# A list scheduler in the builder of an attention and two-layer feed-forward kernel

## The chip, the core and the metric

The kernel runs on one core of a Trainium2 chip. The time is that of one execution on the device, in microseconds (us); the median of 3 runs of the kernel before is 934.12 us (933.48 to 934.25). Engines in the profile: PE is TensorE's matmuls and PEld its weight loads, DVE is VectorE, ACT is ScalarE, POOL is GpSimd, SP is SyncE, which here issues every DMA. Each engine works through its own instructions in the order in which they were written, and waits on semaphores for the others.

## What is computed

Attention with a window of 32 keys to each side and 32 global tokens, for 4 batches and 8 heads of width 64; then a gated layer with an RMS norm in front (width 512, inner width 1536), and a second layer with a squared relu (inner width 2048). There are 2304 tokens. All is f32.

```python
s_ll = np.where(mask, scale * q_l @ k_l.T, -1e9)      # |i - j| <= 32
a_l = softmax(concat([scale * q_l @ k_g.T, s_ll]))
out_l, out_g = a_l @ concat([v_g, v_l]), softmax(scale * q_g @ k_all.T) @ v_all
xn = x / sqrt(mean(x * x) + 1e-6) * rms_g
x = (silu(xn @ w_gate) * (xn @ w_val)) @ w_out
h = x @ w_in
out = (s * relu(h) ** 2 + b) @ w_out2
```

## The kernel before, in words

**Groups.** The tokens are worked in 5 groups, three of 512 and two of 320 (one batch each; then halves of batch 3 with the global tokens of two batches). For each group, layer one has 12 blocks g (gate), 12 blocks v (value) and 12 blocks o (out), and layer two 16 blocks i and 16 blocks p. A block is 4 slices of 3 matmuls (`mm3`, lines 751 to 758), since each operand is split into a high and a low fp32r half: high weights by high input (line 752), high by low (753), low by high (754). A slice of 128x512 comes out in PSUM: g, v and i go to one of two banks `m`, o and p add up in four banks `acc0` to `acc3`.

**What follows a block.** In layer one, ACT makes `sg` = silu of g (line 829), DVE multiplies it with v (`a`, line 841), ACT casts the high half `h` (line 156), and DVE makes the low half (line 162). In layer two, ACT makes `r` = relu (line 858), DVE `t` (859), ACT the high half of `h` (861), DVE the low half (862). The block o or p that reads `h` stands one block i, or one g and v, later on PE. At the end of layer one, ACT and DVE carry the four `acc` to `y` (lines 787, 789).

**Weights.** Each pair of two blocks is 1 MB. There are 34 pairs. In group 0 each comes as raw 64-bit data into one of 4 buffers `wr` (line 174), and is converted by three ACT instructions (`ce` line 205, `cv` line 195, the cast `wt` line 223) and four of DVE (lines 206, 208, 209, 224). Most are then stored to DRAM (`wsc`, line 218), from where the later groups load them (line 279) into one of 7 buffers `wt`; 10 of the 34 are converted again in group 1 instead (`AGAIN`).

**Attention and norm beside it.** While a group runs through its layers, the attention of the next one is computed between the blocks, two heads' pairs at a time (`pair_steps`): scores `st_s`, global scores `st_g`, exponentials `st_e`, transposes `st_t` and `st_tg`, values `st_v`, all through one PSUM bank pair `at`. Then `build_steps` makes the next group's input `x`: squares, `root` (one over the root by a start value and four Newton steps, 15 small DVE instructions in `inv_rms`, lines 495 to 501), the scaling `u` (527) and the transposes `turn`; in two groups also `gsq` and `gnorm`, which do the same for the global tokens on 128x64.

**What sets the order.** The builder writes blocks in a fixed sequence. Between slices `tick` takes a step of attention, of the building or of the conversions when a count of matmul time (`sched["t"]`) has gone past a pace or a lag given with the step; a step is written whole. In group 0 the framework's own scheduler then arranges PE, ACT and DVE with priorities (`hp`) and a few pinned rows (`in_line`), so that slices of different blocks are mixed; from group 1 on (line 812) the written order is the order. SP's order is the order of the calls.

Of the kernel before, what the change touches and what calls it, by code (L numbers as in the profile page):

```python
# [21 lines left out]
T = B * ST  # L22
# [47 lines left out]
W_LEAD = 5  # L70
C_LEAD = 4
# [5 lines left out]
def attn_moe_kernel(ctx: ExitStack, tc: tile.TileContext, q, k, v, w, cst, out):  # L77
# [63 lines left out]
    slots = []  # L141
    for gi in range(len(GROUPS)):
        slots += [(1, gi, f) for f in range(F1)] + [(2, gi, f) for f in range(F2)]
    wt, wraw, wsc, left = {}, {}, {}, {}
    raws, stores = {}, {}
    nraw = [0]
    nload = [PAIRS]
    cnt = {}

    def pick(key, opts):  # L150
        cnt[key] = cnt.get(key, -1) + 1
        return opts[cnt[key] % len(opts)]

    def cpy(e, out_, in_):
        if e == "A":
            A.copy(out=out_, in_=in_)
        else:
            V.tensor_copy(out=out_, in_=in_)

    def hl(dst_h, dst_l, src, eh):  # L160
        cpy(eh, dst_h, src)
        return V.tensor_tensor(out=dst_l, in0=src, in1=dst_h.bitcast(F32), op=ALU.subtract)

    def w_tile(n):
        wt[n] = w_p.tile([128, 2, 2, 512], F32R, tag="w", name="wt")
        left[n] = 2
        return wt[n]

    def load_raw():
        if nraw[0] < len(RAW):  # L170
            n = RAW[nraw[0]]
            nraw[0] += 1
            wraw[n] = wr_p.tile([128, 2, 512], I64, tag="wr", name="wr")
            raws[n] = nc.sync.dma_start(out=wraw[n], in_=w[n % PAIRS])
# [6 lines left out]
    table = []  # L181

    def tabled(xs):
        in_line(table + xs)
        table[:] = [xs[-1]]

    def conv_begin(n, halves=False):
        raw = wraw.pop(n)
# [24 lines left out]
    def keep(n, wn):  # L213
        m = n % PAIRS
        if n == m and m in AGAIN:
            return
        wsc[m] = dr_p.tile([128, 2, 2, 512], F32, name=f"wsc{m}")
        stores[n] = nc.sync.dma_start(out=wsc[m], in_=wn.bitcast(F32))
# [9 lines left out]

    def conv(n):
        g, a, d = conv_begin(n)  # L230
        in_line(a)
        for c, y in (("A", a[0]), ("V", d[0])):
            if c in recent:
                in_line([recent[c], y])
        conv_end(n, g)

    def conv_steps(n):
        raw = wraw.pop(n)
        hi = raw.bitcast(I32).rearrange("p j (n t) -> p j n t", t=2)[:, :, :, 1]
        odd = raw.bitcast(I16).rearrange("p j (n t) -> p j n t", t=2)[:, :, :, 1]  # L240
        e = cv_p.tile([128, 2, 512], I32, tag="cv", name="ce")
        g = cv_p.tile([128, 2, 512], F32, tag="cv", name="cv")
        t = g.bitcast(I32)
        wn = w_tile(n)

        def end():
            V.tensor_tensor(out=wn[:, :, 1], in0=g, in1=wn[:, :, 0].bitcast(F32), op=ALU.subtract)
            load_raw()
            keep(n, wn)

        return [(lambda: A.mul(out=g, in_=hi.bitcast(F32), mul=W_SC), 0.0),
                (lambda: A.copy(out=e.bitcast(I16), in_=odd), 1.3),
                (lambda: V.tensor_scalar(out=g, in0=g, scalar1=-W_HI * W_SC, scalar2=W_HI * W_SC, op0=ALU.max,
                                         op1=ALU.min), 0.6),
                (lambda: V.tensor_scalar(out=e, in0=e, scalar1=13, scalar2=-0x7FFFFFF9, op0=ALU.arith_shift_right,
                                         op1=ALU.bitwise_and), 1.3),
                (lambda: V.scalar_tensor_tensor(out=t, in0=t, scalar=3, in1=e, op0=ALU.logical_shift_left,
                                                op1=ALU.bitwise_or), 0.6),
                (lambda: A.copy(out=wn[:, :, 0], in_=g), 1.3), (end, 1.3)]

    def block(gi, b):
        n, j = divmod(gi * 2 * PAIRS + PLACE[b], 2)
        return n, wt[n][:, j]

    def used(n):
        left[n] -= 1
        if left[n]:
            return
        del wt[n], left[n]
        if n + C_LEAD < PAIRS:  # L270
            conv(n + C_LEAD)
        elif n + W_LEAD in RAW[PAIRS:]:
            sched["c"] += conv_steps(n + W_LEAD)
        while PAIRS <= nload[0] <= n + W_LEAD and nload[0] < PAIRS * len(GROUPS):
            m = nload[0]
            nload[0] += 1
            if m in RAW:
                continue
            nc.sync.dma_start(out=w_tile(m).bitcast(F32), in_=wsc[m % PAIRS])

    ut, og_t, raw_u = {}, {}, {}

    def u_tile(b):
        if b not in ut:
            ut[b] = u_p.tile([128, 4, DM], F32, tag="u", name="u")
        return ut[b]

    def og_tile(b):
        if b not in og_t:
            og_t[b] = xg_p.tile([128, 2, 64], F32, tag=f"xg{b}", name="og")  # L290
        return og_t[b]

    def load_qk(i):
        if i >= len(UNITS) or i in raw_u:
            return
# [5 lines left out]
        for t, src, e in ((qr, q, n), (kr, k, m)):  # L301
            d = nc.sync.dma_start(out=t[:, 0:e], in_=src[b, p, :, 0:e])
            if i < 2:
                in_line([raws[4], d])
# [645 lines left out]
```

## Time and profile before

| what | us |
|---|---|
| median of 3 runs | 934.12 |
| the profiled execution | 934.58 |
| its span, first to last instruction | 932.8 |
| PE busy | 912.6 (98%) |
| DVE busy | 470.4 (50%) |
| ACT busy | 423.0 (45%) |
| DMA, share of 16 engines (main queue) | 72.9% |
| granted TensorE clock, mean | 0.998 |

The first 40 us are the attention of the first group, which has nothing to hide it; it is written by the same lines before and after. From 39.8 us on the blocks run: group 0 to 253 us, group 1 to 465, group 2 to 675, group 3 to 807, group 4 to the end. A row of a timeline gives start, duration, engine, line, operation, what it writes and reads, and in brackets the idle time of the engine ahead of it with what ended it. Matmuls overlap: a 128x512 one is shown with 0.39 us and the next begins 0.23 us after it.

### The profile page before, as it was taken

What the parts mean: (1) busy time and instruction counts of PE and PEld (TensorE: products, weight loads), DVE (VectorE), ACT (ScalarE), POOL (GpSimd) and SP (SyncE); (2) the same over time, 40 slices, a digit from 0 to 9 for tenths busy, and PEclk for the clock granted to TensorE, in tenths of its full rate; (3) what the DMA queues carried; (4) which work ended last, traced back from release to release, by engine and by line L of the source; (5) the groups of instructions that cost most, each with busy time, mean ns of one, the idle gap of its engine ahead of it and who ended that gap; (6) DMA issues with size and microseconds to landing.
All of it is one profiled execution on the core that took longest, in us unless ns stands there. A gap on an engine that the chain in (4) does not pass through costs nothing.

```text
span 932.8 us, 16385 instructions
## 1 busy us (share of the span) xinstructions
PE 912.6 (98%) x6942; PEld 778.0 (83%) x6942; DVE 470.4 (50%) x794; ACT 423.0 (45%) x600; POOL 0.6 (0%) x7
## 2 busy tenths in 40 slices
PE   9899998998999999999999999999999999999998
PEld 7677786877878878788778878887899999999998
DVE  5897999979563563556341242344322135311333
ACT  3797987978436336454214115232232233211322
POOL 0000000000000000000000000000000000000000
PEclk9999999999999999999999999999999999999999
DMA  9799999788958887574666654554588787698780
GB/s 362 290 422 420 350 371 389 248 352 328 350 183 329 309 318 269 189 285 181 225 237 225 254 189 183 192 195 156 204 314 298 280 298 272 246 335 308 289 294 29
DMA packets 43960, 255.77 MB, mean 274 GB/s; under 512 B 5104, under 2 KB 9456, under 8 KB 15984
## 3 DMA queue, kind: packets, MB, share of 16 engines
q1 hardware_dynamic: 43888, 254.73, 72.9%
q8 instruction: 55, 0.90, 0.4%
q14 instruction: 17, 0.14, 0.0%
HBM read 214.60 MB, written 40.11 MB: 273 GB/s over the span
## 4 chain that ended last, share of the span: by engine, by line
PE 77%; ACT 9%; DVE 8%; DMA 3%; issue 2%; POOL 0%; ACTq 0%; DVEq 0%; POOLq 0%
PE m L752 14%; PE m L753 13%; PE m L754 13%; PE acc L753 9%; PE acc L752 9%; PE acc L754 9%; ACT ce L205 2%; DMA wr<-in_w_dram 2%; ACT cv L195 2%; PE at L366 1%; DMA wsc<-wt 1%; ACT h L861 1%; DVE t L859 1%; DVE wt L224 1%; ACT wt L223 1%
## 5 line engine op out<-in xcount | busy, mean ns | idle before, releaser
L753 PE MATMUL acc<-h,wt 128*128 128x512 f32 (+1 forms) x536 | 192.9, 360 | 1.1 <-DVE h L862 1.1
L754 PE MATMUL acc<-h,wt 128*128 128x512 f32 (+1 forms) x536 | 191.6, 358 | 0.0
L752 PE MATMUL acc<-h,wt 128*128 128x512 f32 (+1 forms) x536 | 187.1, 363 | 3.7 <-ACT h L861 3.6
L752 PE MATMUL m<-x,wt 128*128 128x512 f32 (+1 forms) x480 | 174.2, 363 | 0.7 <-ACT sg L829 0.7
L754 PE MATMUL m<-x,wt 128*128 128x512 f32 (+1 forms) x480 | 171.7, 358 | 0.0
L753 PE MATMUL m<-x,wt 128*128 128x512 f32 (+1 forms) x480 | 171.5, 357 | 0.0
L752 PE MATMUL m<-y,wt 128*128 128x512 f32 (+1 forms) x320 | 115.4, 361 | 6.2 <-DVE t L859 6.2
L753 PE MATMUL m<-y,wt 128*128 128x512 f32 (+1 forms) x320 | 115.1, 360 | 1.6 <-DVE y L789 1.6
L752 PEld LDWEIGHTS acc<-h,wt 128*128 128x128 f32 x536 | 100.4, 188 | 18.9 <-ACT h L861 5.2
L754 PE MATMUL m<-y,wt 128*128 128x512 f32 (+1 forms) x320 | 114.8, 359 | 0.0
L753 PEld LDWEIGHTS acc<-h,wt 128*128 128x128 f32 x536 | 100.7, 188 | 15.4 <-DVE h L862 3.1
L754 PEld LDWEIGHTS acc<-h,wt 128*128 128x128 f32 x536 | 100.6, 188 | 12.8 <-issue 0.2
L841 DVE TENSOR_TENSOR a<-sg,m 128x512 f32<-128x512 f32 (+1 forms) x60 | 36.3, 605 | 144.5 <-PE m L754 131.8
L859 DVE SCALAR_TENSOR_TENSOR t<-m,ct,r 128x512 f32<-128x512 f32 (+1 forms) x80 | 53.3, 668 | 105.9 <-ACT r L858 105.3
L752 PEld LDWEIGHTS m<-x,wt 128*128 128x128 f32 x480 | 90.0, 188 | 14.2 <-issue 1.4
L754 PEld LDWEIGHTS m<-x,wt 128*128 128x128 f32 x480 | 90.1, 188 | 11.6
L753 PEld LDWEIGHTS m<-x,wt 128*128 128x128 f32 x480 | 90.1, 188 | 10.9 <-DVE x L604 0.2
L858 ACT ACTIVATE r<-m 128x512 f32<-128x512 f32 (+1 forms) x80 | 42.4, 532 | 120.3 <-PE m L754 119.8
L829 ACT ACTIVATE sg<-m 128x512 f32<-128x512 f32 (+1 forms) x60 | 32.0, 534 | 126.7 <-PE m L754 126.6
L861 ACT ACTIVATE h<-t,ct 128x512 fp32r<-128x512 f32 (+1 forms) x79 | 52.3, 662 | 60.5 <-DVE t L859 58.2
L862 DVE SCALAR_TENSOR_TENSOR h<-t,ct,h 128x512 fp32r<-128x512 f32 (+1 forms) x79 | 53.1, 672 | 47.1 <-ACT h L861 43.3
L752 PEld LDWEIGHTS m<-y,wt 128*128 128x128 f32 x320 | 60.2, 188 | 14.6 <-DVE t L859 7.2
(163 smaller groups left out, 1032.2 us busy)
## 6 DMA issues: line engine op xcount, KB each, us to landing
wt<-wsc SPq DMA_DIRECT2D x126, 1024.0 KB, 4.9
wr<-in_w_dram SPq DMA_DIRECT2D x44, 1024.0 KB, 7.7
wsc<-wt SPq DMA_DIRECT2D x34, 1024.0 KB, 8.3
vr<-in_v_dram SPq DMA_DIRECT2D x12, 1105.0 KB, 8.3
fk<-in_k_dram SPq DMA_DIRECT2D x12, 784.0 KB, 6.0
fq<-in_q_dram SPq DMA_DIRECT2D x12, 272.0 KB, 6.5
out_dram<-z SPq DMA_DIRECT2D x12, 256.0 KB, 4.8
s_v<-in_v_dram SPq DMA_DIRECT2D x2, 1040.0 KB, 9.8
```

The source lines that it names most:

```text
L195: mul = lambda: A.mul(out=g, in_=hi.bitcast(F32), mul=W_SC)
L205: a = [A.copy(out=e.bitcast(I16), in_=odd), mul()]
L223: a = A.copy(out=wn[:, :, 0], in_=g)
L752: mms = [PE.matmul(out_, lhsT=wh, rhs=xh, start=first, stop=False), PE.matmul(out_, lhsT=wh, rhs=xl, start=False, stop=False), PE.matmul(o ...
L753: PE.matmul(out_, lhsT=wh, rhs=xl, start=False, stop=False),
L754: PE.matmul(out_, lhsT=wl, rhs=xh, start=False, stop=last)]
L829: recent["A"] = A.activation(out=sg[:, :N], in_=gb[:, :N], func=AF.Silu)
L841: V.tensor_tensor(out=a[:, :N], in0=sg[:, :N], in1=vb[:, :N], op=ALU.mult)
L858: A.activation(out=r[:, :N], in_=hb[:, :N], func=AF.Relu)
L859: V.scalar_tensor_tensor(out=t[:, :N], in0=hb[:, :N], scalar=ct[:, C_S:C_S + 1], in1=r[:, :N], op0=ALU.mult, op1=ALU.mult)
L861: recent["A"] = A.activation(out=h[:, 0, :N], in_=t[:, :N], func=AF.Identity, bias=ct[:, C_B:C_B + 1])
L862: recent["V"] = V.scalar_tensor_tensor(out=h[:, 1, :N], in0=t[:, :N], scalar=ct[:, C_B:C_B + 1], in1=h[:, 0, :N].bitcast(F32), op0=ALU.add ...
```

## The change

All of `pick`, `conv`, `conv_steps`, `pair_steps`, `build_steps`, `tick`, `emit_step` and the loop over blocks goes. In their place the builder makes a list of operations (`Op`) for all five groups, each with an engine, a duration in us written into the code, what it waits for, and which buffers it takes and frees (`Ring`). Then a loop takes, again and again, the operation that can start first on PE, ACT, DVE or the DMA queue, by these written durations, and writes it; from the end of the first attention on the written order is the order on all four. `cls` ranks what is ready: 0 for what follows a block, then attention and norm (1.0), conversions (2.0, or 0.5 when their pair is at most 3 pairs ahead of PE); no more than 5 pairs ahead. On ACT and DVE an operation of lower rank is left aside if one of rank 0 would be ready over 1 us (`TOL`) before its end. PE takes blocks in a fixed sequence in halves of 6 matmuls, and between halves an attention step that is ready. The Newton steps of the norm are five operations of three instructions each. On SP, raw loads rank before loads from `wsc`, and stores last.

```diff
-W_LEAD = 5
-C_LEAD = 4
+CAP = 4.0
+AHEAD = 5
+CONV = 2.0
+TOL = 1.0
+NEAR = 3
...
+    def commit(o, t):
...
+        x = o.fn()
...
+        free[o.eng] = t + d - OVER[o.eng]
+        o.done = t + d + LAT[o.eng]
...
+        return Op("Q", 2.6, f, [], [r], cls=1.0, after=[prev]), r
...
+    def mm3(out_, wh, wl, xh, xl, fst, lst):
+        r = PE.matmul(out_, lhsT=wh, rhs=xh, start=fst, stop=False)
+        PE.matmul(out_, lhsT=wh, rhs=xl, start=False, stop=False)
+        PE.matmul(out_, lhsT=wl, rhs=xh, start=False, stop=lst)
+        return r
...
+            o = Op("PE", 2 * mm_us(N), f, pairs[n].ops + h["ops"], recs if f_ == 0 else [],
+                   [pairs[n].w, h["rec"]] + ([] if f_ == 0 else recs))
...
+        def f1():
+            x = V.scalar_tensor_tensor(out=T["t"], in0=T["r"], scalar=-0.5, in1=T["r"], op0=ALU.mult, op1=ALU.mult)
+            V.tensor_tensor(out=T["t"], in0=T["t"], in1=T["m"], op=ALU.mult)
+            V.scalar_tensor_tensor(out=T["r"], in0=T["t"], scalar=1.5, in1=T["r"], op0=ALU.add, op1=ALU.mult)
+            return x
+
+        o = Op("V", 3 * us, f0, deps, [], uses)
+        for _ in range(4):
+            o = Op("V", 3 * us, f1, [o])
+        return o, T
...
+        for x in sorted((x for x in c if x[0] <= t0 + 0.6), key=lambda x: (x[1] if x[0] <= t0 + 0.12 else 5 + x[0], x[2])):
...
+            if k > 0 and any(y[0] > s and y[0] < s + d - TOL for y in crit):
+                continue
+            best = x
+            break
...
+        if a and e:
+            if a[0] <= free["PE"] + 0.05 and a[0] >= s["ok"]:
+                return a
+            if e[0] > free["PE"] + 0.3 and a[0] + 0.4 < e[0]:
+                return a
+            return e
...
+    ctx.enter_context(tc.manual_schedule(engines={x.engine for x in (PE, A, V, nc.sync)}))
...
+        E, (t, _, _, o) = min(c, key=lambda x: x[1][0])
...
+        commit(o, t)
```

Three places in the written order show it. The first is DVE in layer two of group 3, where `gnorm` makes the norm of the global tokens (`msq`, `nt`, `r_` are its small tiles, `t` and `h_` those of a block i). Before, its last part:

```order
L501 SCALAR_TENSOR_TENSOR r_7359<-nt,r_7359 128x64
L499 SCALAR_TENSOR_TENSOR nt<-r_7359 128x64
L500 TENSOR_TENSOR nt<-nt,msq 128x64
L501 SCALAR_TENSOR_TENSOR r_7359<-nt,r_7359 128x64
L562 TENSOR_TENSOR gxn<-at,r_7359 128x256
L564 TENSOR_TENSOR gxn<-gxn,ct 128x256
L162 TENSOR_TENSOR x<-gxn,x 128x4x64
L859 SCALAR_TENSOR_TENSOR t<-m,ct,r 128x320
```

The change, at the same norm:

```order
L1073 SCALAR_TENSOR_TENSOR r_7039<-nt,r_7039 128x64
L802 SCALAR_TENSOR_TENSOR t<-m,ct,r 128x320
L1071 SCALAR_TENSOR_TENSOR nt<-r_7039 128x64
L1072 TENSOR_TENSOR nt<-nt,msq 128x64
L1073 SCALAR_TENSOR_TENSOR r_7039<-nt,r_7039 128x64
L810 SCALAR_TENSOR_TENSOR h_7068<-t,ct,h_7068 128x320
L1071 SCALAR_TENSOR_TENSOR nt<-r_7039 128x64
L1072 TENSOR_TENSOR nt<-nt,msq 128x64
```

`t` and the low half of `h` now stand between Newton steps; before, all 18 instructions of the norm stood in one piece.

The second is DVE at the end of layer one of group 0 (`y` is layer two's input, `mx` and `pm_` belong to attention scores, `ce`, `cv`, `wt` to conversions). Before:

```order
L224 TENSOR_TENSOR wt<-cv,wt 128x2x512
L350 TENSOR_TENSOR at<-at,ct 128x16x32
L351 TENSOR_REDUCE mx<-at 128x8
L789 TENSOR_TENSOR y<-acc,y 128x512 x2
L352 TENSOR_TENSOR pm_106<-at,mx 128x1024
L789 TENSOR_TENSOR y<-acc,y 128x512 x2
```

The change:

```order
L536 TENSOR_SCALAR ce<-ce 128x1024
L545 SCALAR_TENSOR_TENSOR cv<-cv,ce 128x1024
L720 TENSOR_TENSOR y<-acc,y 128x512 x4
L553 TENSOR_TENSOR wt<-cv,wt 128x2x512 x2
L540 TENSOR_SCALAR cv<-cv 128x1024
```

The four parts of `y` are now in one piece, with nothing of attention ahead of them or between them.

The third is PE at the first block o of group 0, the first reader of weight pair 2. Before, the framework put the high weights of all four slices first and the low ones (line 754) after the next block had begun:

```order
L752 MATMUL acc<-h,wt 128x512
L753 MATMUL acc<-h,wt 128x512
L752 MATMUL m<-x,wt 128x512
L753 MATMUL m<-x,wt 128x512
L754 MATMUL acc<-h,wt 128x512 x4
```

The change:

```order
L647 MATMUL acc<-h,wt 128x512
L648 MATMUL acc<-h,wt 128x512
L649 MATMUL acc<-h,wt 128x512
L215 MATMUL at<-fk,fq 32x128 x32
L647 MATMUL acc<-h,wt 128x512
L648 MATMUL acc<-h,wt 128x512
```

The third matmul of each slice now reads the low weights, ahead of the next slice; before, eight matmuls with the high weights came first.

## Rows read from the trace of the kernel before

**Rows 1.** From the page: busy time of each engine, and shares of the chain.

```profile
PE 912.6 (98%) x6942; PEld 778.0 (83%) x6942; DVE 470.4 (50%) x794; ACT 423.0 (45%) x600; POOL 0.6 (0%) x7
...
PE 77%; ACT 9%; DVE 8%; DMA 3%; issue 2%; POOL 0%; ACTq 0%; DVEq 0%; POOLq 0%
```

**Rows 2.** Busy time by stretch: PE, PEld, DVE, ACT, POOL, granted clock, DMA share, GB/s.

```profile
39.78:152.44 112.66, 111.91 (x898) 89.24 (x896) 100.80 (x135) 95.17 (x96) 0.00 (x0) 1.00 0.98 396
152.44:252.60 100.16, 92.61 (x581) 74.93 (x580) 81.96 (x127) 79.30 (x91) 0.00 (x0) 0.98 0.85 319
```

**Rows 3.** Waits of PE: line waited for, us in total, times, longest us.

```profile
PE m L752 <- DVE t L859: 6.2, 3, 3.1
PE acc L752 <- ACT h L861: 3.6, 3, 1.8
PE m L753 <- DVE y L789: 1.6, 2, 1.4
PE acc L753 <- DVE h L862: 1.1, 5, 0.3
...
PE m L752 <- ACT sg L829: 0.7, 2, 0.4
```

**Rows 4.** Timeline of PE, matmuls at waits and behind them.

```profile
208.13 0.50 PE L752 MATMUL m<-y,wt 128*128 128x512 f32 x1 [2.00 <-DVE t L859]
...
233.32 0.50 PE L752 MATMUL m<-y,wt 128*128 128x512 f32 x1 [3.14 <-DVE t L859]
233.65 0.39 PE L753 MATMUL m<-y,wt 128*128 128x512 f32 x1
233.88 0.40 PE L754 MATMUL m<-y,wt 128*128 128x512 f32 x1
...
235.13 0.63 PE L752 MATMUL m<-y,wt 128*128 128x512 f32 x1
235.56 0.63 PE L753 MATMUL m<-y,wt 128*128 128x512 f32 x1
...
373.88 0.50 PE L753 MATMUL m<-y,wt 128*128 128x512 f32 x1 [0.19 <-DVE y L789]
...
644.09 0.49 PE L752 MATMUL acc<-h,wt 128*128 128x512 f32 x1 [1.83 <-ACT h L861]
```

**Rows 5.** Timeline of DVE, the norm of global tokens in group 2.

```profile
636.85 0.22 DVE L495 TENSOR_SCALAR msq<-at 128x64 f32<-128x64 f32 x1 [4.21 <-PE at L559]
...
640.42 0.23 DVE L501 SCALAR_TENSOR_TENSOR r<-nt,r 128x64 f32<-128x64 f32 x1
...
642.53 0.75 DVE L859 SCALAR_TENSOR_TENSOR t<-m,ct,r 128x512 f32<-128x512 f32 x1
```

**Rows 6.** Timeline of ACT and DVE ahead of the wait at 233 us.

```profile
230.87 0.59 ACT L858 ACTIVATE r<-m 128x512 f32<-128x512 f32 x1
...
231.73 0.88 DVE L527 TENSOR_SCALAR u<-u,r 128x512 f32<-128x512 f32 x2
```

**Rows 7.** Groups by line and shape, ACT and DVE: busy, mean ns; idle before.

```profile
L205 ACT COPY ce<-wr 128x2048 int16<-128x2048 int16 x31 | 58.8, 1896 | 0.0
L195 ACT ACTIVATE cv<-wr 128x1024 f32<-128x1024 f32 x34 | 39.2, 1153 | 0.6 <-DMA wr<-in_w_dram 0.6
L223 ACT CAST wt<-cv 128x1024 fp32r<-128x1024 f32 x34 | 35.8, 1053 | 6.2 <-DVE cv L209 6.1
...
L829 ACT ACTIVATE sg<-m 128x512 f32<-128x512 f32 x36 | 21.5, 598 | 74.7 <-PE m L754 74.6
...
L224 DVE TENSOR_TENSOR wt<-cv,wt 128x1024 fp32r<-128x1024 f32 x34 | 41.5, 1220 | 4.1 <-ACT wt L223 4.0
```

**Rows 8.** Timeline of ACT: the last cast of the head.

```profile
41.05 1.07 ACT L223 CAST wt<-cv 128x1024 fp32r<-128x1024 f32 x1
```

**Rows 9.** Timeline of PE in the head: an attention step behind its copy.

```profile
30.37 0.32 PE L366 MATMUL at<-s_w,ptf 128*32 128x65 f32 x8 [0.25 <-ACT ptf L676]
```

**Rows 10.** DMA issues: KB each, median us to landing.

```profile
wr<-in_w_dram SPq DMA_DIRECT2D x44, 1024.0 KB, 7.7
```

More of the change, by code (lines that the diff above doesn't have):

```diff
@@ L227, in conv_end @@
         return a, d
[L229 to L279, printed above, removed]
@@ new lines, in attn_moe_kernel @@
+    pool_ = {"A": [], "V": [], "Q": []}
+    free = {"PE": 0.0, "A": 2.0, "V": 4.0, "Q": 5.0}
+    tab = ["S"]
+    first = {}
+    ends = {}
+    def commit(o, t):
+        d = o.dur
+        if o.tab and o.tab != tab[0]:
+            d += 1.28
+            tab[0] = o.tab
+        for r in o.takes:
+            r.ring.hist.append(r)
+        x = o.fn()
+        if o.eng in first:
+            in_line([first.pop(o.eng), x[0] if isinstance(x, list) else x])
+        free[o.eng] = t + d - OVER[o.eng]
+        o.done = t + d + LAT[o.eng]
+        for r in o.uses:
+            r.n -= 1
+            r.t = max(r.t, o.done)
+        for s in o.succ:
+            s.need -= 1
+            s.ready = max(s.ready, o.done)
+        for s in o.then:
+            s.need -= 1
+        if o.eng != "PE":
+            pool_[o.eng].remove(o)
@@ new lines, in load_op, with f, head_pairs @@
+    def load_op(n, prev):
+        p = Pair()
+        p.w = rec("w")
+        def f():
+            wt[n] = w_p.tile([128, 2, 2, 512], F32R, tag="w", name="wt")
+            return nc.sync.dma_start(out=wt[n].bitcast(F32), in_=wsc[n % PAIRS])
+        p.alloc = Op("Q", 2.6, f, [stored[n % PAIRS]], [p.w], cls=1.5, after=[prev])
+        p.ops = [p.alloc]
+        return p
+    def head_pairs():
+        for n in range(2):
+            p = Pair()
+            p.w = rec("w")
+            R["w"].hist.append(p.w)
+            p.ops, p.alloc, p.begin = [], None, None
+            wt[n] = wt_head[n]
+            wsc[n] = wsc_head[n]
+            pairs[n] = p
+        wraw.update(raw_head)
@@ new lines, in all_pairs @@
+    def all_pairs():
+        head_pairs()
+        raw = {}
+        for n in range(6):
+            r = rec("wr")
+            R["wr"].hist.append(r)
+            raw[n] = (None, r, (-9.0, -9.0, -9.0, -5.0, 0.5, 3.5)[n])
+            if n < 2:
+                r.t = 0.0
+        last = None
+        prev = []
+        for n in range(2, PAIRS * len(GROUPS)):
+            if n in RAW:
+                if n not in raw:
+                    o, r = raw_op(n, last)
+                    last = o
+                    raw[n] = (o, r, -9.0)
+                o, r, t = raw[n]
+                p = conv_ops(n, o, r, [pairs[n - 1].begin if n - 1 in pairs and n - 1 > 1 and n - 1 in RAW else None,
+                                       pairs[n - 1].alloc])
+                p.begin.ready = max(p.begin.ready, t)
+                store_op(n, p)
+            else:
+                p = load_op(n, pairs[n - 1].alloc)
+                p.begin = None
+            pairs[n] = p
@@ L875, in _masks @@
+    assert state["e"] == len(experts) and state["a"] == len(attend) and not any(pool_.values())
 def _masks():
```

1039 lines of the change are left out of this document (652 added, 387 removed).

## The prediction

> **What bounds the kernel now.** I read the shares and the chain first [rows 1]. PE is busy 98% of the span, and 77% of the chain runs over it; DVE and ACT are busy 50% and 45%. So the time is the sum of the matmuls, which the change leaves as they are, and of what PE loses between them. DVE and ACT matter only where they let PE wait. The view by stretch shows where that is likely: in layer one of group 0 DVE is busy 100.80 of 112.66 us and ACT 95.17, with the DMA engines at 0.98 of full use; in layer two of the same group it is 81.96 and 79.30 of 100.16 us [rows 2]. PE loses almost nothing in the first (111.91 of 112.66 busy) and 7.6 us in the second. Behind group 0 the weights are only loaded, and both engines have room.
>
> The waits of PE are the heart of it [rows 3]. They add up to 13.2 us: three for `t` (6.2), three for the high half of `h` (3.6), two for `y` (1.6), five for the low half of `h` (1.1) and two for silu (0.7). These rows leave out the first 40 us, which the change doesn't touch. All are waits for what follows a block; none is for a weight or an attention step.
>
> Why these came late is read on the other two engines. Ahead of the wait of 3.14 us [rows 4], `r` was ready at 231.46, but DVE was in two scalings `u` until 232.6 and began `t` only then [rows 6]. Ahead of the wait of 1.83 us at 644.09 [rows 4], the norm held DVE from 636.85 to 640.65 with 15 small instructions, and DVE reached `t` at 642.53 [rows 5]. The wait of 1.4 us for `y` [rows 3] is at the end of layer one of group 0, where the written order has two attention instructions ahead of `y` and one between its parts. So the order of short instructions costs here, and not a lack of engine time.
>
> **The change part by part.** The sum is made against the profiled execution, 934.58 us with a span of 932.8; it stands 0.46 above the median of 934.12.
>
> *What PE loses now.* The 13.2 us of waits; the restart: the first matmul after a wait is followed by the next 0.33 us later instead of 0.23 (233.32 to 233.65, then 233.88) [rows 4], 0.1 us for each of the 15 waits, 1.5 us; and the clock. After the wait of 3.14 us the matmuls run on at 0.23 us, then a stretch comes in which they stand 0.43 us apart (235.13 to 235.56) [rows 4]: 0.20 us lost for each of four, and about as much again in the transposes behind them, between 0.8 and 1.4 us; I take 1.2. In that stretch the granted clock is at its lower level, 1.2 GHz, and the mean of layer two of group 0 is 0.98 [rows 2]. After the wait of 2.00 us at 208.13 the spacing stays at full speed. Together 15.9 us.
>
> The Trainium skill, "TensorE: Matmul & The Clock Gate", section "What's actually happening", says that the slow clock is the default and that activity releases it, so a pause of PE brings it back. The trace agrees for the wait of 3.14 us and shows nothing of it after 2.00. If the short wait that the change adds at the first block o brought it too, that would take 1.2 us off the sum, and the time would be 925.5; by the rows it is 924.3.
>
> *What goes.* DVE's order now has `t` and `h` between Newton steps, whose pieces are three instructions of 0.26 us, and all `y` ahead of attention. An operation of lower rank may still end up to 1 us after one of rank 0 is ready, but `h` is read only a block later: 12 matmuls of 0.23 us are 2.7 us of room. So the three waits for `t`, the three for the high half of `h` with the low halves behind them, silu, the clock and their restarts go. What stays has its reason in the sequence of blocks: `y` follows the last block o at once, so the 0.19 us that stand even where nothing is in the way (373.88) [rows 4] stay at both ends of layer one, with a restart each 0.6 us; and one first block p, where only one block i lies between, 0.3 us. 15.9 - 0.9 = 15.0 us go.
>
> *What is added, at the first block o.* Its weights, pair 2, must now be whole, low halves too, when the first slice runs. ACT's written order behind the cast of 41.05, which ends at 42.1 [rows 8]: `ce` 1.90, silu 0.60, `cv` 1.15, `ce` of the next pair 1.90, a cast of `h`, as long as a silu, 0.60, its `cv` 1.15, silu 0.60, and then the cast of pair 2, 1.05 [rows 7]. That is 42.1 + 8.95 = 51.1, and DVE's low half 1.22 us more [rows 7], 52.3. PE is there 48 matmuls of 0.23 us after 39.8, at about 51.0, and needs the low half with the third matmul, at 51.5. So 0.8 us are lost; between 0 (if DVE runs ahead of this) and 1.3. The mixing of slices that avoided it is gone.
>
> *What is added, at attention steps.* PE takes an attention step as soon as the written durations say that its input is ready, with 0.05 us to spare; before, lags of 1 to 5 us stood between steps. There are 64 such steps (24 scores and value steps of local pairs, 12 transposes, and 28 of the global tokens and the building). If an input is late, PE waits with all blocks behind it. No such wait stands in the rows after 40 us; the nearest is in the head, where values follow their copy at once: 0.25 us [rows 9]. So 0 to 64 x 0.25 = 16 us. I take 3.4, a little over one step in five, nearer to zero, since a step also has to wait for a boundary of six matmuls, 1.4 us, which gives most of them slack.
>
> *What is moved within group 0.* The first attention pair is written later, behind the conversions, so that about 3 us of DVE and 4 of ACT go from layer one to layer two, where they have 18 and 21 us free [rows 2]. I put 1.0 us on it, between 0 and 3.1, the longest wait that PE has there [rows 3].
>
> *At nothing:* two ACT table loads fewer (ACT isn't the bound), and on SP the stores that now follow raw loads, and the first loads of queries, keys and values, which now stand behind the second store and the next raw loads: the DMA engines work them off beside the blocks, and attention of the next group has a whole group of blocks before it is needed. If that cover goes, it is the second rival.
>
> Sum: 15.0 - 0.8 - 3.4 - 1.0 = 9.8 us less. 934.58 - 9.8 = 924.8 for a profiled execution, 934.12 - 9.8 = **924.3** for the median.
>
> **The rivals.**
>
> *The waits move to attention steps.* For it: nothing in the new order holds reserve; the durations written into it are single numbers. Against: the written ones are within 0.02 us of the rows for conversions (1.9 against 1.896, 1.14 against 1.153, 1.05 against 1.053) [rows 7]. At 0.25 us for nearly every step, 14 us, the gain of 15.0 - 0.8 is used up: about 934, between 932 and 936.
>
> *Late raw loads stop ACT; slower.* The builder counts a raw load with 2.6 us and 2.0 behind it, 4.6 us; the row has 7.7 us from issue to landing [rows 10], and the DMA engines are at 0.98 in layer one of group 0 [rows 2]. An ACT instruction that waits for a raw block holds the silu behind it, and PE with it. A load may be 3.1 us late. It decides where ACT has less room than that: the silu has about 5.4 us (two blocks) before its bank `m` is wanted. So it takes conversions already behind by 2.4 us or more; then each of 28 raw loads of group 0 can cost up to 3.1 us. With seven of them, 21.7 us, the kernel comes to 934.1 - 15.0 + 21.7 = 941, and it is slower from five on. Against it: four raw buffers, a lead of up to 5 pairs (27 us of blocks), and a DMA queue that hides its backlog in the 7.7 us.
>
> The Trainium skill, the same page, section "Architectural detail: the array is 16× 32×32, not 1× 128×128", says that ScalarE and VectorE take their queues strictly in order. The trace agrees (`t` behind `u`, [rows 6]); by it a load that is late would hold silu as said.
>
> *Nothing is added.* Then 934.12 - 15.0 = 919.1, the floor, unless PE's busy time itself shrinks, for which I see no reason.
>
> **How the numbers follow.** Forecast, 919 to 930: 0.69, its middle 924.3. Waits at attention steps, 930 to 936, centre 934: 0.14. Late loads, over 936: 0.14. Below 919: 0.03. The range 919 to 936 holds 0.83. A measurement of this kernel tells 0.2%, 1.9 us, from no change; the bounds are 932.3 and 936.0. Faster: the forecast, what is below it, and a small part of the first rival, 0.72; same: the rest of the first rival, 0.12; slower: late loads and the first rival beyond its price, 0.16.
>
> **What would show it.** In the waits of PE: `t` and the high half of `h` gone or below 1 us each, `y` at 0.2 twice; a wait of about 0.8 us at the first block o near 51 us. If the first rival holds, PE waits for ACT or DVE at lines of attention. If the second, ACT waits for the raw loads, and PE for silu in group 0. In layer two of group 0 the granted clock should be 1.00. The prediction is wrong if PE's waits stay above 10 us, or if they go and the span doesn't follow.

## The result, and the profile after

The changed kernel takes 922.10 us (median of 4, 921.00 to 922.33), the kernel before beside it 934.18 (median of 4, 933.48 to 935.33). The ratio is 0.9867, with a 95% interval of 0.985 to 0.9884. The forecast was 924.3, with a range of 919 to 936. The profiled execution took 922.33 us, with a span of 920.5, against 934.58 and 932.8.

The page after, busy time and the chain that ended last; [rows 1] are its counterpart:

```profile
PE 904.3 (98%) x6942; PEld 773.4 (84%) x6942; DVE 471.4 (51%) x793; ACT 425.5 (46%) x599; POOL 0.6 (0%) x7
...
PE 92%; DMA 3%; DVE 2%; ACT 2%; issue 0%; SPq 0%; DVEq 0%; ACTq 0%
```

DVE and ACT do the same work, and a smaller part of the chain runs over them: PE has 92% of it instead of 77%. The waits of PE from 39 us on (line waited for, us in total, times, longest), against [rows 3]:

```profile
PE at L957 <- ACT pm L249: 2.2, 1, 2.2
PE at L1146 <- DVE x L1130: 1.4, 1, 1.4
PE m L648 <- DVE y L720: 0.9, 1, 0.9
PE at L1118 <- DVE x L1130: 0.5, 2, 0.4
PE acc L648 <- DVE h L810: 0.2, 1, 0.2
```

Fifteen waits of 13.1 us have become six of 5.2. None is for `t`, for silu or for the high half of `h`. Four of the six stand in front of attention and norm steps (lines 957, 1118, 1146), where none stood before.

Layer one and layer two of group 0 (length, busy time and instructions of each engine, granted clock, share of DMA), against [rows 2]:

```profile
39.20:146.58 107.38, 105.18 (x580) 85.22 (x579) 96.67 (x125) 96.67 (x94) 0.00 (x0) 0.98 0.99 398
146.58:249.23 102.65, 102.39 (x977) 82.71 (x975) 89.34 (x140) 82.23 (x96) 0.00 (x0) 1.00 0.88 336
```

In layer two the 7.6 us that PE lost are down to 0.3, and the granted clock is 1.00. Layer one now has the largest wait and a clock of 0.98. DVE is busy 4 us less in layer one and 7 us more in layer two; the two stretches don't hold quite the same attention as before.

**Where the wait of 2.18 us comes from.** PE, DVE and ACT around it (start, duration, engine, line, operation, output and inputs, and in brackets the idle time ahead with what ended it):

```profile
138.68 0.39 PE L649 MATMUL acc<-h,wt 128*128 128x512 f32 x1
141.25 1.93 PE L957 MATMUL at<-ct,pm 128*128 128x128 f32 x8 [2.18 <-ACT pm L249]
142.83 0.78 PE L647 MATMUL acc<-x,wt 128*128 128x512 f32 x1
143.40 0.63 PE L648 MATMUL acc<-x,wt 128*128 128x512 f32 x1
143.83 0.63 PE L649 MATMUL acc<-x,wt 128*128 128x512 f32 x1
```

```profile
134.05 0.37 DVE L895 COPY qf<-fq 64x32 f32<-64x32 f32 x2 [1.38 <-DMA fq<-in_q_dram]
136.69 0.37 DVE L895 COPY qf<-fq 64x32 f32<-64x32 f32 x2 [2.27 <-DMA fq<-in_q_dram]
137.09 0.69 DVE L745 TENSOR_TENSOR a<-sg,m 128x512 f32<-128x512 f32 x1
```

```profile
137.81 0.62 ACT L749 CAST x<-a 128x512 fp32r<-128x512 f32 x1 [3.13 <-DVE a L745]
...
140.14 2.00 ACT L249 ACTIVATE pm<-pm 128x1024 f32<-128x1024 f32 x2
```

DVE stood 1.38 and 2.27 us for a load of q, with `a` behind it; ACT stood 3.13 us for `a`, with a conversion (`ce`) and the exponentials `pm` behind that; PE stood 2.18 us for `pm`. The rows also show what a wait costs. From the matmul at 138.68 to the step at 141.25 there are 2.57 us, where 0.23 is the distance of two matmuls: 2.34 us lost, for 2.18 of idle time. And behind it the clock is at its lower level, 1.2 GHz (granted clock 0.50 between 142 and 144): transposes of 1.93 us (eight of the same shape take 1.06 at 244.24) and matmuls 0.43 us apart.

The two loads of q left SP at 124.67 and 125.98:

```profile
124.67 0.39 SPq L846 DMA_DIRECT2D fq<-in_q_dram  x1
...
125.98 0.89 SPq L846 DMA_DIRECT2D fq<-in_q_dram  x1
```

From issue to the copy that waits it is 9.4 us for the first and 10.7 for the second. The builder counts 0.7 + 2.0.

**The wait of 1.41 us.** ACT and DVE carry `x` out of `at`, in layer two of group 3:

```profile
737.67 1.21 ACT L1126 ACTIVATE x<-at,ct 128x256 fp32r<-128x256 f32 x3
739.43 0.47 ACT L1126 ACTIVATE x<-at,ct 128x256 fp32r<-128x256 f32 x1 [0.55 <-DVE x L1130]
...
738.91 0.48 DVE L1130 SCALAR_TENSOR_TENSOR x<-at,ct,x 128x256 fp32r<-128x256 f32 x1 [0.61 <-ACT x L1126]
739.94 1.27 DVE L1130 SCALAR_TENSOR_TENSOR x<-at,ct,x 128x256 fp32r<-128x256 f32 x3 [0.54 <-ACT x L1126]
```

DVE's first eviction starts only behind ACT's third, and ACT's fourth only behind DVE's first. In the written durations the two run side by side. So DVE ends 1.4 us after the time at which PE comes for the bank.

### The profile page after: what moved, and what is told of

It is laid out like the page before. It is cut to its first block, busy times and chain, and to the rows that moved or that the text cites. A ratio compares the mean times of both kernels' runs of the same rounds, so it can differ in the third digit from the quotient of the medians.

```text
span 920.5 us, 16382 instructions
## 1 busy us (share of the span) xinstructions
PE 904.3 (98%) x6942; PEld 773.4 (84%) x6942; DVE 471.4 (51%) x793; ACT 425.5 (46%) x599; POOL 0.6 (0%) x7
## 4 chain that ended last, share of the span: by engine, by line
PE 92%; DMA 3%; DVE 2%; ACT 2%; issue 0%; SPq 0%; DVEq 0%; ACTq 0%
PE m L647 17%; PE m L649 16%; PE m L648 16%; PE acc L647 11%; PE acc L649 11%; PE acc L648 11%; DMA wr<-in_w_dram 2%; PE at L215 1%; PE at L252 1%; PE at L957 1%; DMA fq<-in_q_dram 1%; PE at L935 1%; PE at L992 1%; PE at L1118 1%; PE acc L341 1%; DMA s_r<-in_k_dram 1%
## 5 line engine op out<-in xcount | busy, mean ns | idle before, releaser
L745 DVE TENSOR_TENSOR a<-sg,m 128x512 f32<-128x512 f32 (+1 forms) x60 | 36.4, 607 | 136.5 <-PE m L649 133.7
L648 PEld LDWEIGHTS m<-x,wt 128*128 128x128 f32 x480 | 90.2, 188 | 10.8 <-DVE x L293 0.3
L529 ACT COPY ce<-wr 128x2048 int16<-128x2048 int16 x42 | 79.7, 1897 | 0.4 <-DVE wt L553 0.3
```

The source lines that it names most:

```text
L529: return A.copy(out=T["e"].bitcast(I16), in_=odd)
L648: PE.matmul(out_, lhsT=wh, rhs=xl, start=False, stop=False)
L745: return V.tensor_tensor(out=T["a"][:, :N], in0=T["sg"][:, :N], in1=vt["m"][:, :N], op=ALU.mult)
```

## Experiments

One table for all of them. The 4080 matmuls of blocks, in order of time, are cut into five groups of 816, with everything else that PE does between; each column is the time from the first matmul of a group to the first of the next, from the starts in PE's timeline. (The last block p of a group stands behind the first blocks of the next, so the cut is by count and not by block.) Group times are those of the one profiled execution, the medians those of all. Attention has no share in group 4.

| kernel | median us | ratio to before | group 0 | 1 | 2 | 3 |
|---|---|---|---|---|---|---|
| before | 934.2 | | 218.9 | 208.8 | 209.0 | 132.1 |
| after | 922.1 | 0.9867 [0.985, 0.9884] | 212.9 | 208.3 | 206.5 | 129.8 |
| e1 before, Newton in pieces | 927.8 | 0.9937 [0.9925, 0.995] | 218.0 | 207.0 | 206.4 | 130.4 |
| e2 Newton whole | 922.9 | 0.9885 [0.9871, 0.9899] | 211.4 | 208.3 | 206.5 | 131.1 |
| e3 nothing left aside | 922.1 | 0.9873 [0.986, 0.9885] | 211.8 | 208.3 | 206.5 | 129.6 |
| e4 no ranks | 951.0 | 1.0185 [1.0172, 1.0198] | 239.3 | 209.1 | 207.9 | 129.6 |
| e5 all loads later | 923.0 | 0.9886 [0.9873, 0.9899] | 213.3 | 208.3 | 206.5 | 129.8 |
| e6 reserve at every step | 928.5 | 0.995 [0.9937, 0.9963] | 218.8 | 207.8 | 206.4 | 130.3 |
| e7 both | 927.3 | 0.9934 [0.9923, 0.9946] | 216.8 | 207.8 | 206.4 | 130.3 |
| e8 two ranks | 951.2 | 1.0188 [1.0173, 1.0203] | 242.0 | 208.3 | 206.5 | 129.8 |
| e9 q, k, v later | 919.7 | 0.9847 [0.9832, 0.9862] | 209.6 | 208.3 | 206.5 | 129.8 |
| e10 attention earlier | 920.7 | 0.986 [0.9843, 0.9876] | 210.1 | 208.3 | 206.5 | 129.8 |
| e11 e9 with reserve at two steps | 920.8 | 0.9859 [0.9844, 0.9874] | 209.6 | 207.7 | 206.4 | 132.0 |
| e12 what follows a block ranked low | 956.6 | 1.0234 [1.021, 1.0259] | 229.4 | 210.0 | 217.3 | 135.9 |

From its first to its last matmul group 4 takes 120.2 us in every one of them. The change gains 6.0 us in group 0, 0.6, 2.5 and 2.3 in the next three, and nothing in the last.

### What do the pieces of Newton bring?

One part of the change alone, in the kernel before, for the norms that are made in groups 1 to 3:

```diff
-        for _ in range(4):
-            V.scalar_tensor_tensor(out=t, in0=r, scalar=-0.5, in1=r, ...)
-            V.tensor_tensor(out=t, in0=t, in1=m, op=ALU.mult)
-            V.scalar_tensor_tensor(out=r, in0=t, scalar=1.5, in1=r, ...)
+        def newton():
+            ...
         steps.append((root, 1.6))
+        if gi > 1:
+            steps += [(lambda: S["nw"](), 0.7)] * 4
...
-            steps += [(gsq, 4.6), (gnorm, 2.0)]
+            steps += [(gsq, 4.6), (gnorm, 2.0)] + [(lambda: S["gw"](), 0.7)] * 4 + [(gend, 0.7)]
```

> The kernel before with one part of the change alone: the Newton steps in pieces, where the norms of groups 2, 3 and 4 are made (the order of group 0 and of the norm of group 1 stays as it was). Theory: the waits of PE for h behind these norms (444.94, 445.73, 644.09, 644.88, 797.49, 798.08 us: 0.76 + 0.29 + 1.83 + 0.29 + 1.01 + 0.17 = 4.35 us, and up to 0.6 us of restarts) go, and the kernel comes to 934.2 - 4.4 = 929.8 us; the waits in group 0 (1.40, 1.02, 2.00, 3.14) stay. Rival: the pieces alone do little, since the written order sets t and h behind other work all the same; then 933 to 935 us, with waits of 1 us or more for h left in groups 1 to 3.

927.8 us, 5.7 us less than before (4.7 to 7.0 by the interval). Its waits of PE from 39 us on:

```profile
PE m L762 <- DVE t L869: 4.6, 3, 2.0
PE m L763 <- DVE y L799: 1.6, 2, 1.4
PE m L762 <- ACT sg L839: 0.7, 2, 0.4
PE acc L764 <- DVE wt L224: 0.5, 1, 0.5
PE acc L763 <- DVE h L872: 0.4, 2, 0.2
```

The six waits for `h` behind the norms are gone, and the `t` that are left are all in group 0. Groups 1 to 3 take 6.2 us less (1.8, 2.7, 1.7), for 4.35 us of waits: each wait cost more than its idle time. That is more than the whole change gains in these groups, 5.4.

The other way round, the norm in one piece in the changed kernel:

```diff
+        def f01():
+            x = f0()
+            for _ in range(4):
+                f1()
+            return x
+
-        o = Op("V", 3 * us, f0, deps, [], uses)
-        for _ in range(4):
-            o = Op("V", 3 * us, f1, [o])
+        o = Op("V", 15 * us, f01, deps, [], uses)
```

> The changed kernel with the 15 instructions of each norm as one operation of 15 pieces again (2.5 us on 128x4, 3.45 us on 128x64). Theory: the rule that leaves lower ranks aside finds no gap of 3.45 us, so the norm runs where nothing better fits, t and h come 1 to 2.5 us late at the two global norms, and the kernel is 1 to 3 us slower, 923 to 925 us, with waits for t or h of 1 us or more near 640 and 796 us. Rival: the room of one block (2.7 us) hides it, and the time stays within 0.5 us of 922.1.

922.9 us, 0.75 above the change in the median, with intervals that overlap. Only group 3 shows it, 131.1 instead of 129.8: its norm on 128x64 holds DVE from 745.36 to 749.2, and PE waits 0.49 and 0.25 us for `h` at 750. In groups 1 and 2 nothing is lost. So pieces and order are not two gains that add up. In groups 1 to 3 either will nearly do: with the scheduler even the whole norm finds a place where it costs little, and in the old order the pieces let `t` and `h` in. The theory had 1 to 3 us and both global norms, the rival 0; it is 1.3 us in one group.

In group 0, up to the norm, PE, ACT and DVE have the same order in e2 as in the change, so e2 shows the wait of 2.18 us a second time:

```profile
135.51 0.36 DVE L895 COPY qf<-fq 64x32 f32<-64x32 f32 x2 [2.26 <-DMA fq<-in_q_dram]
140.06 1.09 PE L957 MATMUL at<-ct,pm 128*128 128x128 f32 x8 [0.82 <-ACT pm L249]
```

The second copy runs 1.2 us earlier than in the change (136.69), PE waits 0.82 us instead of 2.18, and the granted clock stays at 1.00. So the size of this wait goes with the load and changes from one execution to the next.

### Which rule of the order brings the gain?

```diff
-        crit = [x for x in c if x[1] == 0.0]
+        crit = []
```

> The changed kernel without the rule that leaves an operation of lower rank aside when one of rank 0 would be ready over 1 us before its end; what is ready is still ranked. Theory: little of the gain hangs on it, since only instructions of over 1 us (ce 1.90, cast and cv 1.05 to 1.22 us) are concerned and t, h have a block of room: 922 to 925 us, with new waits of under 1 us in group 0. Rival: it carries the gain; then the waits for t, h and silu come back and the kernel is at 930 us or more.

922.07 us: in the time, the rule that leaves lower ranks aside brings nothing here. In the profile `y` waits more often (0.34, 0.79 and 0.88 us), and `h` twice (0.29 and 0.36), but the 2.18 us are missing. That can't be put down to the rule: ACT, DVE and PE have another order around that step, and the second load of q came 1.3 us earlier (its copy runs at 135.41).

Next, no ranks at all, then two of them (what follows a block, and the rest):

```diff
-        ... key=lambda x: (x[1] if x[0] <= t0 + 0.12 else 5 + x[0], x[2])):
+        ... key=lambda x: (x[0], x[2])):                                              # e4, with crit = []
+        ... key=lambda x: (min(x[1], 0.5) if x[0] <= t0 + 0.12 else 5 + x[0], x[2])): # e8
```

> The changed kernel with no ranks on ACT and DVE at all: what can start first by the written durations goes first, then the order in which the operations were made. Theory: the ranks carry the gain; the waits for t, h, y and silu come back, 5 to 15 us, 927 to 937 us, most of them in group 0, where DVE and ACT are busy 80 to 90% of the time. Rival: an order by earliest start is enough, and the time stays within 2 us of 922.1.

> The changed kernel with two ranks on ACT and DVE: what follows a block first, then all other work (attention, norm and conversions) as it was made, by its start. Theory: what follows a block carries the gain, and the order among the rest costs little: 921 to 926 us, against 951 us with no ranks at all. Rival: with conversions no longer behind attention, the attention of group 1 piles up at the end of group 0 (by the written order its steps stand closer there), and PE waits for it or for its input x: 930 to 945 us.

951.0 and 951.2 us. The theory behind e4, that the rank of what follows a block carries the gain, doesn't explain it: e8 keeps that rank and loses as much. Both lose in group 0 alone; groups 1 to 3 are those of the change, within 1.4 us. Layer one and two of group 0 in e4, then in e8:

```profile
39.10:164.80 125.70, 115.41 (x898) 92.50 (x896) 108.71 (x144) 106.00 (x103) 0.00 (x0) 0.95 0.96 384
164.80:275.50 110.70, 102.20 (x659) 80.63 (x657) 79.89 (x122) 77.19 (x90) 0.00 (x0) 0.94 0.73 275
```

```profile
39.20:140.40 101.20, 101.18 (x564) 82.63 (x562) 94.59 (x118) 93.82 (x91) 0.00 (x0) 1.00 1.01 409
140.40:275.50 135.10, 112.14 (x930) 89.18 (x929) 92.57 (x147) 85.04 (x98) 0.00 (x0) 0.87 0.76 292
```

In e4 layer one is longer: attention runs early, ahead of conversions, and PE waits there for `fk` (6.3 us) and silu (4.0), and in layer two for `h`. In e8 conversions run first, layer one is the shortest of all (101.20, PE busy throughout), and attention piles up behind it. When the blocks of group 0 are done (at 237 us), PE goes through the rest of attention and the norm one step at a time:

```profile
240.80 1.97 PE L935 MATMUL at<-fk,qf 128*64 128x512 f32 x4 [3.50 <-DVE pm L925]
245.70 1.97 PE L957 MATMUL at<-ct,pm 128*128 128x128 f32 x8 [2.77 <-ACT pm L249]
...
268.55 2.43 PE L1118 MATMUL at<-ct,u 128*128 128x128 f32 x8 [7.50 <-DVE u L1099]
```

So in group 0 there is a second chain beside the blocks: loads of q, k and v, the attention of group 1, its norm and `x`. It has to be done when the blocks are. The ranks of attention against conversions hold this balance; without it 29 us are lost.

What the rank of what follows a block is worth by itself:

```diff
-        crit = [x for x in c if x[1] == 0.0]
+        crit = []
-        ... key=lambda x: (x[1] if x[0] <= t0 + 0.12 else 5 + x[0], x[2])):
+        ... key=lambda x: (x[1] or 1.2 if x[0] <= t0 + 0.12 else 5 + x[0], x[2])):
```

> The changed kernel with what follows a block ranked behind attention and behind conversions of near pairs on ACT and DVE, and without the rule that leaves lower ranks aside (which alone changed nothing: 922.07 us). Theory: the rank of what follows a block is what took the waits for t and h away; they come back, 5 to 15 us, 927 to 937 us, most in group 0, and silu and t wait by 1 us or more. Rival: earliest start does it already, and the rank of attention against conversions, which cost 29 us when it was dropped, is all that matters: 921 to 925 us.

956.6 us, beyond the theory's 937. Its waits:

```profile
PE acc L648 <- DVE h L810: 6.6, 4, 3.8
PE at L215 <- DMA fk<-in_k_dram: 6.3, 1, 6.3
PE at L1118 <- DVE x L1130: 5.9, 2, 3.0
PE at L1146 <- DVE x L1130: 5.5, 2, 3.1
```

Here groups 2 and 3 lose too, 10.8 and 6.1 us. The wait of 3.8 us for `h` is at the first global norm, where all Newton pieces, `gxn` and its multiplication run ahead of the low half. So in groups 1 to 3 what follows a block mustn't stand behind the norm; first by rank, or first by the time at which it can start (e4), doesn't matter. In group 0 this run mixes both faults, and what each costs there was not taken apart. No wait for `t` or silu stands in its group 0, though the theory had them come back.

### Does the change lack reserve?

Three edits for the waits that are left: every load counted 4 us later, attention steps on PE only 1.5 us after they are ready by the written durations, and both.

```diff
-    LAT = {"PE": 0.2, "A": 0.07, "V": 0.07, "Q": 2.0}
+    LAT = {"PE": 0.2, "A": 0.07, "V": 0.07, "Q": 6.0}      # e5, e7
...
-                t = o.start(free["PE"])
+                t = o.start(free["PE"] - 1.5)              # e6, e7
                 if t is not None:
-                    t = max(t, s["begin"] + (12.0 if g == 0 else 0.0))
+                    t = max(t + 1.5, s["begin"] + (12.0 if g == 0 else 0.0))
```

> The changed kernel with the builder counting every load as there 4 us later (6.0 instead of 2.0 us behind its issue time). Theory: the wait of 2.18 us at 141.25 for the exponentials pm, with the slow clock behind it (0.75 us) and the 0.8 us that the transposes run longer, comes from DVE standing 1.38 and 2.27 us for the load of fq in its written order; with the load counted later the copy qf stands behind other work, no wait of PE over 1 us is left in group 0, and the kernel is 2 to 4 us faster than 922.1: 918 to 920 us. Rival: DVE's wait for the load is only one of several things late there, or conversions now start later by 4 us and take the place; then 921 to 924 us, with another wait of over 1 us in layer one of group 0.

> The changed kernel with attention steps on PE only 1.5 us after the written durations say that the input is ready. Theory: the waits at attention steps (0.16, 0.39, 1.41 us, and most of the 2.18 us) come from the missing reserve; they go, and the kernel comes to 918 to 921 us. Rival (what the prediction's first rival has as its price, taken the other way round): each of the 64 steps starts a block later, the attention of a group is done later, and its last steps or the next group's input are waited for; then 923 us or more, with waits for x or at at the ends of groups.

> Both of the last two edits together. Theory: the two act on different waits and add up, 917 to 919 us, and PE waits less than 2.5 us in all behind the first 40 us (y 0.9, h 0.2, little else). Rival: they take away the same 2.18 us, and the kernel is no faster than the better of the two alone.

All three miss the theory. In e5 (923.0) the 2.18 us are gone and group 0 is no shorter: raw weights count as late too, conversions in layer one start later (the 18th cast at 138.8 instead of 133.7), and the scaling `u` of the next input begins at 240.15 instead of 237.17. The end of group 0 gives it back:

```profile
246.47 1.06 PE L1118 MATMUL at<-ct,u 128*128 128x128 f32 x8 [1.52 <-DVE x L1130]
250.38 1.15 PE L215 MATMUL at<-fk,fq 64*32 64x128 f32 x64 [1.45 <-issue]
```

In e6 (928.5) the reserve, paid at each step, delays the second chain: `u` runs at 245.32, when the last block is nearly done, and PE has nothing left to do beside it.

```profile
245.69 0.39 PE L649 MATMUL acc<-h,wt 128*128 128x512 f32 x1
...
247.40 1.16 PE L1118 MATMUL at<-ct,u 128*128 128x128 f32 x6 [0.82 <-DVE u L1099]
251.67 1.07 PE L1118 MATMUL at<-ct,u 128*128 128x128 f32 x6 [3.11 <-DVE x L1130]
```

The rival of e6 holds, and e7 sits between its parts.

Then the same cause with a smaller edit: only the loads of q, k and v are counted 4 us later.

```diff
-        o.done = t + d + LAT[o.eng]
+        o.done = t + d + LAT[o.eng] + (4.0 if o.eng == "Q" and o.cls in (0.8, 1.2) else 0.0)
```

> The changed kernel with the loads of q, k and v alone counted 4 us later by the builder (raw weights stay at 2.0 us). In the written order little moves: on DVE the copy qf stands behind a, cv, wt and the low half of the last h instead of in front of them, ACT's order is the same. Theory: the wait of 2.18 us at 141.25 and the slow clock behind it come from DVE standing 1.38 and 2.27 us for the load of q in front of these; they go, and with them 2.18 us of waiting, 0.93 us of slow matmuls and 0.85 us of slow transposes: 918 to 920 us. Rival: what the run with all loads later showed, that layer two of group 0 gives it back, since the attention and the input of the next group end with the last blocks of group 0; then 921 to 923 us, with a wait of 1 us or more for x or u near 245 us.

919.71 us (919.29 to 920.06), all runs below all those of the change, and 0.9847 of before; the interval (0.9832 to 0.9862) still overlaps that of the change by a little. ACT's order is the same, and on DVE `qf` moves behind `a` and the low half:

```profile
134.01 0.69 DVE L745 TENSOR_TENSOR a<-sg,m 128x512 f32<-128x512 f32 x1 [0.46 <-PE m L649]
...
136.35 0.69 DVE L752 TENSOR_TENSOR x<-a,x 128x512 fp32r<-128x512 f32 x1
136.95 0.74 DVE L895 COPY qf<-fq 64x32 f32<-64x32 f32 x4
```

`qf` waits for nothing, and group 0 is 3.3 us shorter than in the profile of the change (1.8 shorter than in e2, where the load came earlier). The wait for `y` that this uncovers is 0.43 us. So the load of q did cause the 2.18 us, and the slow clock is gone with them; the size was as expected. This is the fastest kernel of the study, near the 919.1 that the forecast gave for the case in which nothing is added.

Two more on the second chain. e10 lets attention begin 6 instead of 12 us into group 0:

```diff
-                    t = max(t, s["begin"] + (12.0 if g == 0 else 0.0))
+                    t = max(t, s["begin"] + (6.0 if g == 0 else 0.0))
```

> The changed kernel with the attention of group 1 free to start 6 us instead of 12 us into group 0. Theory: in group 0 the attention and the input of the next group are a second chain that ends with the last blocks; 1.4 us more room at its start lets it end earlier, and the kernel is 0 to 2 us faster, 920 to 922 us. Rival: the start isn't what holds it (loads or the ranks are), and the kernel is the same or, with the loads of q and k waited for earlier, slower: 922 to 925 us.

920.65 us, with an interval (0.9843 to 0.9876) that overlaps that of the change; in the profile, its fastest execution, group 0 is 2.8 us shorter, and DVE waits 0.55 us for the load of q instead of 1.38 and 2.27. It agrees with the theory and doesn't settle it, since the order around the load of q moved too.

e11 adds to e9 a reserve at the two kinds of steps where waits are left:

```diff
+            o.slack = 0.5 if gi > 1 and p0 else 0.0      # transposes of the next input
...
+            o.slack = 1.4                                # first step of the global norm
...
-                t = o.start(free["PE"])
+                x = getattr(o, "slack", 0.0)
+                t = o.start(free["PE"] - x)
```

> The edit on the loads of q, k and v, and a reserve on PE for two kinds of steps alone: 1.4 us at the first step of the global norm, 0.5 us at the second transposes of an input from group 2 on. Theory: the waits of 1.41 and 0.39 us at these steps go as well, 1.8 us and up to 0.5 us of restarts, since their attention has room there: 916.5 to 918.5 us if the first edit gives 918 to 920, 920 if it gives nothing. Rival: as with a reserve for all steps, a later wait (h behind the global norm, 1.49 us there) takes their place, and the time is that of the first edit alone.

920.84 us, 1.1 above e9. The wait of 1.4 us at line 1146 is gone, and another stands there:

```profile
738.87 0.41 PE L647 MATMUL acc<-h,wt 128*128 128x320 f32 x1 [1.48 <-ACT h L807]
```

`t` stands behind the four evictions of `x` on DVE. They are what is late, and PE waits for DVE at the next thing it needs from it, whatever that is. Idle time alone doesn't explain that group 3 is 2.2 us longer than in e9 (132.0 against 129.8): 1.48 and 0.17 us stand here, 1.40 there. Behind these waits the clock is at its lower level, which it isn't in e9:

```profile
741.00:743.50 2.50, 2.50 (x16) 2.38 (x14) 0.04 (x1) 0.38 (x1) 0.00 (x0) 0.50 0.25 102
```

Evictions that don't wait on one another were not tried.

## Why the prediction was right

The result is 2.2 us below the forecast, inside its range. By steps (the first three take time off, the others put it on), idle time being the waits and the rest worked out from starts in PE's timeline of the two profiled executions:

| step | forecast us | shown us |
|---|---|---|
| waits of before that go | 13.2 - 0.6 | 13.1 - 1.05 = 12.1 |
| what a wait costs beside its idle time, restarts | 1.5 - 0.3 | 4.1 - 0.65 = 3.5 |
| slow clock of before | 1.2 | 0.9 in matmuls, 0.7 in transposes |
| added: first block o | 0.8 | 0 |
| added: attention steps | 3.4 | 4.1 of idle time, 0.7 beside it |
| added: slow clock behind one of them | none | 0.9 in matmuls, 0.8 in transposes |
| moved within group 0 | 1.0 | nothing of its own |
| sum | -9.8 | -10.7 |
| not in the sum | | -1.6 |

That the sums are so near is partly luck: what goes is 17.2 us instead of 15.0, what is added 6.5 instead of 5.2, and the two errors offset each other.

**What goes.** As said: `t`, silu and the high half of `h` no longer wait, `y` stays at 0.88 us and one low half at 0.17. The `y` of group 0, forecast at 0.2, doesn't wait; that of group 1 does, because DVE is in a low half of `wt` for 1.22 us when `y` becomes ready (368.69 to 369.83).

The size was off: a wait is dearer than its idle time. A matmul is shown with 0.39 us and the next starts 0.23 after it, so the idle time in the view begins 0.16 us after the moment when PE could have gone on. At 13 of the 15 waits of before, where a matmul stands ahead, this is 0.16 to 0.27 us each, 2.65 in all; the forecast counted only the 0.1 us behind the wait. The Trainium skill, "TensorE: Matmul & The Clock Gate", section "Single matmul latency", gives a single bf16 matmul at the full clock a constant of about 166 ns over its columns. The row of the fp32r matmul here is near it, 0.39 - 0.23 = 0.16, though the ends of matmuls in the profile are modelled.

**The reason given for it** was partly wrong. The forecast leaned on Newton in pieces and on the rule that leaves lower ranks aside. e3 shows no gain of the rule in the time; e2 that the pieces are worth 1.3 us in one group, once the order is there. What does it in groups 1 to 3 is that `t` and `h` aren't placed behind the norm (e1, e12). In group 0, e4 and e8 show that the balance of attention and conversions has to be kept, of which the forecast didn't speak; without it far more is lost than the change gains. Which rule took away the waits for `t` in group 0 isn't shown: no run of the new builder, whatever its ranks, has one.

**First block o.** 0.8 us were forecast, none came. ACT's cast of pair 2 ends at 49.62 instead of 51.1, DVE's low half at 50.89, and PE, at the first block o from 50.52 on, has its first matmul with a low half of the weights (line 649) at 50.97, without a wait:

```profile
48.55 1.07 ACT L550 CAST wt<-cv 128x1024 fp32r<-128x1024 f32 x1
...
49.66 1.23 DVE L553 TENSOR_TENSOR wt<-cv,wt 128x1024 fp32r<-128x1024 f32 x1
...
50.97 0.46 PE L649 MATMUL acc<-h,wt 128*128 128x512 f32 x1
```

The sum added durations, but an ACT instruction starts 0.08 to 0.12 us before the one ahead ends (`cv` at 47.03, `h` from 46.51 for 0.64): some 0.9 us over the row of eight instructions. The other 0.6 is the head, below.

**Attention steps.** 3.4 us were spread over a dozen steps. Of 64 steps four wait, and one of them takes over half. So the size was right by chance: the price isn't a small one per step, it is a late input now and then, passed on in strict order, and the largest one changes with the load (0.82 us in e2). For the largest it is the mechanism of the second rival, with a load of q in the place of a raw one. The forecast had a load up to 3.1 us later than counted; these two were 6.7 and 8.0 us later, 9.4 and 10.7 us where 2.7 were counted. The builder also keeps up to 4 us (`CAP`) between one attention step and the next, which the forecast left out; what that is worth was not tried. The Trainium skill, "DMA: Bandwidth & Descriptors", section "Anatomy of one DMA — SWDGE (gpsimd) path", puts a transfer at about 2.0 us and its bytes at 436 GB/s, on that path; an estimate by it for the 272 KB of a load of q is 2.6 us. Here, on SP's queue with the DMA engines at 0.99, the measured times differ, and a builder that counts such a figure writes the copy too early.

**Clock.** Layer two of group 0 is at 1.00 as forecast; layer one pays instead. What the slow clock of before cost was put too low, at 0.8 to 1.4 us. The matmuls behind the wait of 3.14 us lost 0.9, and the eight transposes behind them 0.7, from their start to that of the next matmul: 1.49 us instead of 0.82 in the change at 244.24.

```profile
236.41 1.73 PE L533 MATMUL at<-ct,u 128*128 128x128 f32 x8
```

**Not in the sum:** 1.6 us. The head is 0.6 us shorter (39.20 to 39.78), on unchanged code; in the runs of this study it is between 38.9 and 39.8, so it isn't the change. Behind the last matmul 0.3 us less pass (3.35 to 3.65). The other 0.7 us were not traced further.

## What to carry to other kernels

A hand-written order has two faults that look alike in the waits: short urgent work behind long work, which either pieces or another order cures, and a second chain that must end with the first, which only shows when it is late; look for its last step before moving anything ahead of it. Reserve costs at the end of the chain what it saves in the middle, so put it only where an input is really late, here at three kinds of loads, and use durations from the profile, transfers under load above all. Price a wait at its idle time and the overlap it breaks.

## What the runs showed of the chip

**The same wait, with and without a slow clock.** In the profile of before, PE waits 2.00 us at 208.13 and runs on at full speed [rows 4]. In e1, with the same order in group 0, the same wait of 2.00 us is followed by matmuls at the lower level, 1.2 GHz (granted clock 0.50 between 209 and 211):

```profile
208.69 0.79 PE L762 MATMUL m<-y,wt 128*128 128x512 f32 x1 [2.00 <-DVE t L869]
209.28 0.63 PE L763 MATMUL m<-y,wt 128*128 128x512 f32 x1
209.71 0.63 PE L764 MATMUL m<-y,wt 128*128 128x512 f32 x1
```

There it costs some 1.6 us. The wait of 3.14 us at 233.32, which had the slow clock in before, is 1.59 us in e1 and has none. In e11 waits of 1.48 and 0.17 us close together are followed by it. So a wait of 2 us may or may not bring it, and the length alone doesn't tell: the forecast went by the one row of 2.00 us. The Trainium skill, "TensorE: Matmul & The Clock Gate", section "What's actually happening", says that activity releases the slow clock. The runs agree: from 40 us to the last matmul, each stretch at the lower level stands at or behind a wait of PE.

**Load times spread.** The median of a load of q is 6.6 us in the page of after, and the two that mattered took 9.4 and 10.7; in e2, with the same order, the second took 9.4. A median of issue to landing is not what a strict order has to survive.
